# Query-major exponentials 384 wide with a quarter of the keys turned by DMA, the dP matmuls around the burst, and half of TensorE's turns by DMA

## The chip, the cores and the metric

The kernel runs on one core of one Trainium2 chip. The metric is the device time of one execution in microseconds. Three runs of the kernel before took 2671.75, 2677.37 and 2682.45 us.

## What is computed

The reference is a gated mix of a multi-head attention block and a state-space convolution, forward and backward: the output and the gradients of twelve inputs. The change touches the attention alone:

```python
B, S, D, H = 1, 2048, 576, 32          # Dh = 18
scores = jnp.einsum("bhqd,bhkd->bhqk", q, k) * (Dh ** -0.5)
p = _softmax(scores, axis=-1)
o = jnp.einsum("bhqk,bhkd->bhqd", p, v)
# backward (vjp): dv = p^T do;  dp = do v^T;  ds = p * (dp - delta);  dq = ds k;  dk = ds^T q
```

## The kernel before

The program has three stretches: projections, norms and gates (to about 123 us of the span); the attention loop, forward and backward (123 to 2087 us); and the convolution's gradients with the output matmuls (to the end). The engines' order is written by hand: the schedule is manual, each engine runs its instructions in the order in which the code issues them, and engines meet only at semaphores.

Attention works on 8 groups of 4 heads and 4 blocks of 512 queries: 32 units (g, b). The loop `for G in range(NTOT + OFF + 24)` takes 32 steps for a unit (NTOT = 1024 steps of forward work); the backward work of a unit follows its forward work by OFF = 39 steps, so that one step holds forward work of one unit and backward work of an earlier one. G2 = G - OFF counts the backward steps. A step does:

- P1: two matmuls on 32 rows of the array each (two heads), K against Q, give scores key-major, 128 keys x 512 queries a head. ACT takes the exponential of both at once (128x1024) into a tile PT. PT feeds the output matmuls accO (four heads, every other step) and, 39 steps later, ds.
- P3: the same scores for the backward unit once more, but query-major: 128 queries x 512 keys, two heads. ACT takes their exponential (128x1024) into eb. eb feeds dV.
- P2: two matmuls V against dO give dP, one head each into a PSUM tile of its own (two buffers, tag dP). DVE multiplies each by PT into ds (key-major, 128x512 a head, four heads to a tile).
- a burst: per eight steps (one key block of 512 keys, kq) a dV burst in two halves (steps slot 0 and 1; 16 matmuls from eb, first a filler matmul), a dQ burst in two halves (slots 2 and 3; from ds), a dK burst in two halves (slots 5 and 6; from dsT), and in slots 4 and 7 a turn on TensorE. All of them write one PSUM buffer (tag accB), which DVE empties after each second half or turn (`evs`).

dK needs ds with queries on the partitions, dsT. Heads 0 to 2 of each ds tile are turned by a DMA transpose that SP issues (line L1406); the fourth head is turned by TensorE against the identity (turn_p, L1097) and copied by DVE (L1102) for most tiles. `by_pe(p)` says how many of the two tiles of pair p (p = 0 to 7 in a unit) TensorE turns:

```python
return {NPF: 0, NPF + 1: 1}.get(p, 2)
```

With NPF = 5 that is 2, 2, 2, 2, 2, 0, 1, 2: 13 of a unit's 16 tiles.
Where TensorE turns the fourth head the DMA turn is 128x1536, else 128x2048. The two PSUM tiles of tag S (two buffers of two banks) alternate between P1 and P3, so P1 of a step waits for the exponential of P1 of the step before, and P3 likewise.

Beside this, SP's queue issues the loads of K, V, Q and their turned forms, and the turns gT of finished gradients (one of dQ a unit, eight of dV and dK in the last unit of a group). POOL runs the basis of the convolution throughout the loop (et, eG, eT, Eo and the store E_d; about the same amount a step, by a table of estimated costs), and, for the attention, dOa and prod once a unit and the packing of finished gradients (dtk, dqkv_d). DVE's reduce (L1057) waits once a unit for POOL's prod, and POOL's dOa for DVE's reciprocal rl.

Of the kernel before, what the change touches and what calls it, by code (L numbers as in the profile page):

```python
# [11 lines left out]
BF = mybir.dt.bfloat16  # L12
# [5 lines left out]
P = 128  # L18


def build(tc, aps, dbg_aps=None, stages=("s1", "attn", "post", "s4", "final")):
# [40 lines left out]
    with ExitStack() as gctx:  # L62
# [63 lines left out]
        woT = [eds.tile([P, 2, 512], BF, tag="eb", bufs=8, name="eb").rearrange("p a b -> p (a b)")[:, 0:D] for _ in range(DC)]  # L126
# [823 lines left out]
        if "attn" in stages:  # L950
            KB = 512
            NQ = S // KB
            TPQ = KB // P
            DA = HP
            NFILL = {"V": 1, "Q": 0, "K": 0}
            with ExitStack() as ctx:
                ctx.enter_context(tc.manual_schedule(engines={mybir.EngineType.PE, mybir.EngineType.Activation, mybir.EngineType.DVE, mybir.EngineType.Pool, mybir.EngineType.SP}))
# [177 lines left out]

                def dv_half(g, b, kq, h, acc):
                    U = UN[(g, b)]
                    for ii in (2 * h, 2 * h + 1):
                        for j in range(4):
                            mm(acc[HP * j:HP * (j + 1), :], lhsT=U["dOa"][:, ii, j, :], rhs=U["eb"].pop((kq, ii, j)),  # L1140
                               start=(ii == 0), stop=(ii == 3), tile_position=(0, HP * j))

                    def ev():
                        if b == 0:
                            DKV[("v", g, kq)] = work.tile([P, KB], F32, tag="dvacc", bufs=4, name="dvacc")
                            nc.vector.tensor_copy(DKV[("v", g, kq)], acc)
# [4 lines left out]
                        nc.vector.tensor_tensor(o_, a_, acc, op=A.add)  # L1151
                    return ev
# [136 lines left out]
                for G in range(NTOT + OFF + 24):  # L1289
# [18 lines left out]
                    if r1:  # L1308
                        g, b, i, j0 = r1
                        T = grp_t[g]  # L1310
                        ps = s_pair("P1")
                        for x in range(2):
                            row(ps[:, x, :], T["KaT", i // TPQ][:, (i % TPQ) * P:(i % TPQ + 1) * P], T["QaT", b], j0 + x)
                        rows.append(("P1", g, b, i, j0, ps))
                    evs = []
                    slot = (G2 + 1) % 8
                    m_ = (G2 - (7, 8, 8, 8, 8, 8, 8, 0)[slot]) // 8
                    if ("f1", G) in todo:
                        acc = accB("accF")
                        evs.append(todo.pop(("f1", G))[0](acc))  # L1320
                        e_done[0] += 1.4
                    elif G == NST + 5:
                        evs.append(turn(*do_tile(UN[units[0]])))
                    elif 0 <= m_ < NTOT // 8:
                        u_, kq = divmod(m_, NQ)
                        g, b = units[u_]
                        if slot in SLOTS:
                            nm, burst, h = SLOTS[slot]
                            if h == 0:
                                acc = accB("acc" + nm)  # L1330
                                fill(acc, NFILL[nm])
                                burst(g, b, kq, 0, acc)
                            else:
                                evs.append(burst(g, b, kq, 1, acc))
                                if nm == "Q" and kq == NQ - 1:
                                    at(("pre", G + 2), lambda g=g, b=b: store_grad(UN[(g, b)].pop("dqa"), g, 0, b * TPQ))
                                elif nm in "KV" and b == NQ - 1:
                                    at(("pre", G + 2), lambda g=g, kq=kq, nm=nm: store_grad(DKV.pop((nm.lower(), g, kq)), g, 1 + "KV".index(nm), kq * TPQ))
                        else:
# [5 lines left out]
                            evs.append(turn(t_, o_))  # L1345
                    if r2:
                        g, b, s2 = r2
                        T = grp_t[g]
# [8 lines left out]
                        i2 = s2 // 2  # L1357
                        for x in range(2):
                            j2 = 2 * (1 - par_) + x
                            ps = apsp.tile([P, KB], F32, tag="dP", bufs=2, name="ps_P2")  # L1360
                            row(ps, T["VaT", i2 // TPQ][:, (i2 % TPQ) * P:(i2 % TPQ + 1) * P], U["dOaT"].rearrange("p t q -> p (t q)"), j2)
                            rows.append(("P2", g, b, i2, j2, ps))
# [16 lines left out]
                    if 1 <= G <= 2 * NT:  # L1379
                        do_half(G - 1)  # L1380

                    for e_ in evs:
                        e_()
                    for (kind, g, b, i, j, ps) in rows:
                        U = UN[(g, b)]
                        if kind == "P1":
                            U["PT"][i, j // 2] = pt_tile()
                            nc.scalar.activation(U["PT"][i, j // 2], ps, ACT.Exp)  # L1388
                        elif kind == "P3":
                            e = eds.tile([P, 2, KB], BF, tag="eb", bufs=8, name="eb")  # L1390
                            for x in range(2):
                                U["eb"][(i[0], i[1], j + x)] = e[:, x, :]
                            nc.scalar.activation(e, ps, ACT.Exp)  # L1393
                        else:
                            if i not in U["ds"]:
                                U["ds"][i] = eds.tile([P, 4, KB], BF, tag="ds", bufs=5, name="ds")
                                U["dsn", i] = 0
                            nc.vector.tensor_tensor(U["ds"][i][:, j, :], ps, U["PT"][i, j // 2][:, j % 2, :], op=A.mult)  # L1398
                            U["dsn", i] += 1
                            nj = 3 if by_pe(i // 2) >= 2 - i % 2 else 4  # L1400
                            if U["dsn", i] == nj:
                                p = i // 2
# [472 lines left out]
```

## Time and profile before

| | |
|---|---|
| Median of three runs (range) | 2677.37 us (2671.75 to 2682.45) |
| Profiled execution, first to last instruction (span) | 2673.6 us; its own time outside the profiler is not listed apart |
| Mean granted TensorE clock | 0.968 |
| PE, DVE, ACT, POOL busy | 2405.5, 2294.7, 2352.0, 1830.1 us |
| eb and PT exponentials | 1024 each; 1070 and 1075 ns |
| ds multiplies (DVE) | 2048; 683 ns |
| DMA | 486.63 MB, 182 GB/s |

The span is what the sums are made against; it lies 3.8 us under the median. Times in the profile are microseconds, or ns for the mean of one instruction; "<-" stands between output and inputs; "idle before" is the engine's idle time ahead of such instructions, and what ended it. A recorded instruction overlaps its neighbour on the same engine somewhat, so that a mean duration is longer than the pace.

### The profile page before, as it was taken

How to read it: one execution, taken by the hardware profiler on the slowest of the kernel's cores; microseconds unless marked ns; L12 is line 12 of the kernel's file. 1: busy time of each engine (PE TensorE's matmuls, PEld its weight loads, DVE VectorE, ACT ScalarE, POOL GpSimd, SP SyncE). 2: the span in 40 equal slices, each digit the busy share in tenths (PEclk: the TensorE clock that was granted, in tenths of full speed). 3: DMA queues.
4: the chain of work that ended last, by engine and by line, in shares of the span. 5: the costliest groups of instructions: out<-in, count | busy, mean ns of one | idle time of the engine just before them, and what ended most of it. 6: DMA issues, size and time to landing. Idle time of an engine off the chain costs nothing.

```text
span 2673.6 us, 69952 instructions
## 1 busy us (share of the span) xinstructions
PE 2405.5 (90%) x27411; PEld 1134.6 (42%) x27411; DVE 2294.7 (86%) x4090; ACT 2352.0 (88%) x2744; POOL 1830.1 (68%) x2845
## 2 busy tenths in 40 slices
PE   8999999998889898889898999989988699999999
PEld 4433333333333333333333333333232489998756
DVE  5748999999889999889899999999897499999964
ACT  5589999999999999999999999999996489999321
POOL 0388878888888888888878888887931135555431
PEclk9989999999999999999999999999896699999999
DMA  7747889879979978997898899779668979998996
GB/s 232 202 114 152 150 171 177 162 156 181 169 151 172 185 157 163 173 167 152 165 179 157 157 172 169 154 164 181 134 136 174 224 229 262 260 263 250 269 255 136
DMA packets 1155478, 486.63 MB, mean 182 GB/s; under 512 B 1071062, under 2 KB 1108551, under 8 KB 1152843
## 3 DMA queue, kind: packets, MB, share of 16 engines
q1 hardware_dynamic: 1108346, 339.13, 64.3%
q0 software_dynamic: 44784, 137.52, 19.2%
q10 hardware_dynamic: 2016, 5.51, 0.7%
q8 instruction: 214, 3.51, 0.6%
q14 instruction: 118, 0.96, 0.1%
HBM read 146.27 MB, written 93.80 MB: 90 GB/s over the span
## 4 chain that ended last, share of the span: by engine, by line
ACT 39%; PE 28%; DVE 22%; issue 6%; DMA 3%; POOL 2%; SPq 1%; ACTq 0%; DVEq 0%; POOLq 0%
ACT eb L1393 23%; ACT PT L1388 14%; PE ps_P L30 8%; DVE ds L1398 7%; DVE tz L733 3%; DVE wab L753 3%; PE accV L30 2%; PE ps_dx L30 2%; PE turn_p L1097 2%; DVE tz L736 2%; PE accK L30 2%; DVE HG L738 2%; PE yp L30 2%; DVE Rw L758 1%; DVE dvacc L1151 1%
## 5 line engine op out<-in xcount | busy, mean ns | idle before, releaser
L1398 DVE TENSOR_TENSOR ds<-ps_P,PT 128x512 bf16<-128x512 f32 x2048 | 1312.5, 683 | 127.8 <-PE ps_P L30 87.3
L1393 ACT ACTIVATE eb<-ps_P 128x1024 bf16<-128x1024 f32 x1024 | 1095.7, 1070 | 44.3 <-PE ps_P L30 44.2
L1388 ACT ACTIVATE PT<-ps_P 128x1024 bf16<-128x1024 f32 x1024 | 1099.6, 1075 | 11.0 <-PE ps_P L30 9.5
L30 PE MATMUL ps_P<-dOaT,VaT_g 32*128 32x512 bf16 x2048 | 583.1, 390 | 30.8 <-DVE ds L1398 15.4
L506 POOL TENSOR_TENSOR et<-eG,eT 128x448 f32<-128x448 f32 x576 | 542.9, 963 | 10.7
L30 PE MATMUL ps_P<-QaT_g,KaT_g 32*128 32x512 bf16 x2048 | 404.7, 387 | 126.6 <-ACT PT L1388 122.2
L30 PE MATMUL ps_P<-KaT_g,QaT_g 32*128 32x512 bf16 x2048 | 408.9, 392 | 2.0 <-ACT eb L1393 1.4
L506 POOL TENSOR_TENSOR Eo<-et,et 128x448 bf16<-128x448 f32 x288 | 327.2, 1136 | 20.8
L30 PEld LDWEIGHTS <-KaT_g 32*128 32x128 bf16 x2048 | 147.4, 91 | 456.1 <-issue 438.2
L30 PEld LDWEIGHTS <-QaT_g 32*128 32x128 bf16 x2048 | 115.7, 91 | 288.6 <-issue 266.7
L30 PE MATMUL accV<-eb,dOa 128*32 128x512 bf16 x2048 | 185.6, 396 | 26.8 <-ACT eb L1393 26.5
L30 PE MATMUL accO<-PT,Vtok_g 128*32 128x512 bf16 x2048 | 207.9, 395 | 0.1
L30 PE MATMUL accK<-dsT,Qtok_g 128*32 128x256 bf16 x4096 | 165.3, 283 | 21.3 <-DMA dsT<-ds 19.9
L30 PE MATMUL accQ<-ds,Ktok_g 128*32 128x512 bf16 x2048 | 161.9, 394 | 2.2 <-DVE dvacc L1151 1.9
L30 PEld LDWEIGHTS <-Vtok_g 128*32 128x32 bf16 x2048 | 52.8, 93 | 222.6 <-issue 222.6
L1102 DVE COPY dsT<-turn_p 128x1024 bf16<-128x1024 bf16 (+1 forms) x216 | 139.2, 644 | 3.4 <-PE turn_p L1097 3.4
L1097 PE MATMUL turn_p<-ident_bf,ds 128*128 128x128 bf16 x1664 | 136.2, 225 | 1.4 <-DVE gb L1169 0.8
L672 ACT COPY E1e<-etp 128x1024 bf16<-128x1024 bf16 x132 | 125.4, 1063 | 2.7 <-PE etp L671 2.7
L30 PEld LDWEIGHTS <-Qtok_g 128*32 128x32 bf16 x4096 | 88.6, 97 | 87.8 <-issue 57.9
L506 POOL TENSOR_TENSOR et<-eT 128x32 f32<-128x32 f32 (+3 forms) x288 | 116.2, 424 | 11.4
L1097 PEld LDWEIGHTS <-ds 128*128 128x128 bf16 x1664 | 98.9, 100 | 50.2 <-issue 50.0
L1075 POOL COPY dtk<-gT 128x288 bf16<-128x288 bf16 x96 | 40.9, 426 | 107.6 <-DMA dqkv_d<-dtk 47.2
(295 smaller groups left out, 3731.0 us busy)
## 6 DMA issues: line engine op xcount, KB each, us to landing
E_d<-Eo POOLq DMA_DIRECT2D x144, 256.0 KB, 3.3
E1n<-E_d POOLq DMA_DIRECT2D x30, 1024.0 KB, 6.6
T0w<-Kp_d SPq DMA_DIRECT2D x18, 1024.0 KB
xs<-xb_d POOLq DMA_DIRECT2D x28, 512.0 KB, 9.9
dsT<-ds SPq DMA_TRANSPOSE x512
dqkv_d<-dtk POOLq DMA_DIRECT2D x96, 72.0 KB, 4.3
Md_d<-mst SPq DMA_DIRECT2D x18, 288.0 KB
skw<-Md_d SPq DMA_DIRECT2D x72, 64.0 KB
```

What stands on the lines that cost most here:

```text
L30: return nc.tensor.matmul(out, lhsT=lhsT, rhs=rhs, start=start, stop=stop, **kw)
L506: nc.gpsimd.tensor_tensor(out, a, b, op=op)
L672: copy(E_[:, 4 * q:4 * q + 4], pt_)
L733: nc.vector.tensor_tensor(tz[x], HG[:, :, k - 1].unsqueeze(1).to_broadcast([P, 2, 2, n, CB]), ZZ.unsqueeze(3).to_broadcast([P, 2, 2, n, CB ...
L736: nc.vector.tensor_tensor(tz[x][:, 0], tz[x][:, 0], UVk[:, :, :, k, :], op=A.add)
L738: nc.vector.tensor_tensor(HG[:, :, k], tz[x][:, 0], tz[x][:, 1, ::-1], op=A.add)
L753: nc.vector.tensor_tensor(wab, h_, w_, op=A.mult)
L1097: nc.tensor.transpose(pt_[:, x, qb, :], t_[:, qb * P:(qb + 1) * P], ident_bf)
L1102: (nc.scalar.copy if NTOT <= now[0] < NTOT + OFF else nc.vector.tensor_copy)(o_(), pt_[:, x:x + n])
L1388: nc.scalar.activation(U["PT"][i, j // 2], ps, ACT.Exp)
L1393: nc.scalar.activation(e, ps, ACT.Exp)
L1398: nc.vector.tensor_tensor(U["ds"][i][:, j, :], ps, U["PT"][i, j // 2][:, j % 2, :], op=A.mult)
```

## The change

It does four things. P3 and its exponential cover the first 384 of each 512 keys (KT); the last 128 keys of a block come from the forward's PT tile of those keys, which SP turns by DMA into PTt (two turns a key block, each 128x1024 for two heads; two buffers), issued at the start of steps G2 = 8 kq + 1 and + 2. The dV burst takes both: 384 columns from eb and 128 from PTt. The two dP matmuls of a step are split: the first goes ahead of the burst, right behind P1, the second stays after P3; on DVE the burst's eviction goes between the two multiplies. And `by_pe` lets TensorE turn only tiles of even pairs (7 of 16 a unit), the rest goes by DMA.

```diff
-        woT = [eds.tile([P, 2, 512], BF, tag="eb", ...)[:, 0:D] for _ in range(DC)]
-        dO_st = [eds.tile([P, 2, 512], BF, tag="eb", bufs=8, name="eb") for _ in range(3)]
+        woT = [eds.tile([P, 2, 384], BF, tag="eb", ...)[:, 0:D] for _ in range(DC)]
+        dO_st = [eds.tile([P, 2, 384], BF, tag="eb", bufs=8, name="eb") for _ in range(3)]
...
+            KT = KB - P
+            TURNED = (0, 1)
...
-                    return {NPF: 0, NPF + 1: 1}.get(p, 2)
+                    return {NPF + 1: 1}.get(p, 2) if p % 2 == 0 else 0
...
+                def turn_p(u, kq, pair):
+                    U = UN[u]
+                    t_ = U["PTt", kq, pair] = work.tile([P, 2 * TPQ, P], BF, tag="PTt", bufs=2, name="PTt")
+                    nc.sync.dma_start_transpose(out=t_, in_=U["PT"][kq * TPQ + 3, pair].rearrange("p x q -> p (x q)"))
...
                 def dv_half(g, b, kq, h, acc):
-                    for ii in (2 * h, 2 * h + 1):
+                    def stored(ii):
                         for j in range(4):
-                            mm(acc[HP * j:HP * (j + 1), :], lhsT=U["dOa"][:, ii, j, :], rhs=U["eb"].pop((kq, ii, j)),
+                            mm(acc[HP * j:HP * (j + 1), 0:KT], lhsT=U["dOa"][:, ii, j, :], rhs=U["eb"].pop((kq, ii, j)),
                                start=(ii == 0), stop=(ii == 3), tile_position=(0, HP * j))
+                    def turned(ii):
+                        for j in range(4):
+                            mm(acc[HP * j:HP * (j + 1), KT:KB], lhsT=U["dOa"][:, ii, j, :], rhs=U["PTt", kq, j // 2][:, j % 2 * TPQ + ii, :],
+                               start=False, stop=False, tile_position=(0, HP * j))
+                    stored(2 * h)
+                    turned(2 * h)
+                    turned(2 * h + 1)
+                    stored(2 * h + 1)
...
+                for u_ in range(NU):
+                    for kq_ in range(NQ):
+                        for x_, pair_ in enumerate(TURNED):
+                            at(("pre", u_ * NST + OFF + 8 * kq_ + 1 + x_), lambda u_=u_, kq_=kq_, pair_=pair_: turn_p(units[u_], kq_, pair_))
...
+                    if r2:
+                        p2(0)
                     evs = []
...
-                            row(ps[:, x, :], T["QaT", b][:, ii * P:(ii + 1) * P], T["KaT", kq], jo + x)
+                            row(ps[:, x, 0:KT], T["QaT", b][:, ii * P:(ii + 1) * P], T["KaT", kq][:, 0:KT], jo + x)
                         rows.append(("P3", g, b, (kq, ii), jo, ps))
...
+                        p2(1)
...
-                            e = eds.tile([P, 2, KB], BF, tag="eb", bufs=8, name="eb")
+                            e = eds.tile([P, 2, KT], BF, tag="eb", bufs=8, name="eb")
-                            nc.scalar.activation(e, ps, ACT.Exp)
+                            nc.scalar.activation(e, ps[:, :, 0:KT], ACT.Exp)
...
                             nc.vector.tensor_tensor(U["ds"][i][:, j, :], ps, U["PT"][i, j // 2][:, j % 2, :], op=A.mult)
+                            if j % 2 == 0:
+                                for e_ in evs:
+                                    e_()
```

How it moves instructions, at three places. On TensorE, in the first step with backward work (ps_P is a score or dP tile; "<-KaT_g,QaT_g" after QaT_g weights is P3, "<-dOaT,VaT_g" is P2):

```order
-L30 LDWEIGHTS QaT_g
-L30 MATMUL ps_P_1941<-KaT_g,QaT_g 128x512
-L30 LDWEIGHTS QaT_g
-L30 MATMUL ps_P_1941<-KaT_g,QaT_g 128x512
-L30 LDWEIGHTS VaT_g
-L30 MATMUL ps_P_1944<-dOaT,VaT_g 128x512
+L30 LDWEIGHTS VaT_g
+L30 MATMUL ps_P_1941<-dOaT,VaT_g 128x512
+L30 LDWEIGHTS QaT_g
+L30 MATMUL ps_P_1943<-KaT_g,QaT_g 128x384
+L30 LDWEIGHTS QaT_g
+L30 MATMUL ps_P_1943<-KaT_g,QaT_g 128x384
```

One dP matmul has moved ahead of the P3 pair (and, where there is a burst, ahead of it), and the pair is 384 wide.

On DVE, from the eviction of a dV burst to the turn four steps on, before:

```order
L1398 TENSOR_TENSOR ds<-ps_P_11227,PT 128x512
L1146 COPY dvacc<-accV 128x512
L1398 TENSOR_TENSOR ds<-ps_P_11250,PT 128x512
L1398 TENSOR_TENSOR ds<-ps_P_11252,PT 128x512
L1398 TENSOR_TENSOR ds<-ps_P_11285,PT 128x512
L1398 TENSOR_TENSOR ds<-ps_P_11287,PT 128x512
L1164 TENSOR_SCALAR dqa<-accQ 128x512
L1398 TENSOR_TENSOR ds<-ps_P_11319,PT 128x512
L1398 TENSOR_TENSOR ds<-ps_P_11321,PT 128x512
L1102 COPY dsT<-turn_p 128x2x512
```

And in the changed kernel:

```order
L1425 TENSOR_TENSOR ds<-ps_P_11651,PT 128x512
L1163 COPY dvacc<-accV 128x512
L1425 TENSOR_TENSOR ds<-ps_P_11672,PT 128x512
L1425 TENSOR_TENSOR ds<-ps_P_11695,PT 128x512
L1425 TENSOR_TENSOR ds<-ps_P_11709,PT 128x512
L1425 TENSOR_TENSOR ds<-ps_P_11732,PT 128x512
L1181 TENSOR_SCALAR dqa<-accQ 128x512
L1425 TENSOR_TENSOR ds<-ps_P_11745,PT 128x512
L1425 TENSOR_TENSOR ds<-ps_P_11765,PT 128x512
L1425 TENSOR_TENSOR ds<-ps_P_11770,PT 128x512
```

Each eviction now stands between the two multiplies of its step (11651 and 11672), and the copy of the turn in slot 4 is gone.

On SP, over some twelve steps of one unit, before (a ds tile of 12 blocks is three heads, of 16 four; x is the number in a row):

```order
L1071 DMA_TRANSPOSE gT<-gb 128x4x128
L1406 DMA_TRANSPOSE dsT<-ds 128x12x128 x3
L993 DMA KaT_g<-QKV_d 128x1x512
L1006 DMA QaT_g<-QKV_d 128x512
L1406 DMA_TRANSPOSE dsT<-ds 128x12x128 x4
L1010 DMA_TRANSPOSE Qtok_g<-QKV_d 128x4x128
```

And in the changed kernel:

```order
L1073 DMA_TRANSPOSE gT<-gb 128x4x128
L1436 DMA_TRANSPOSE dsT<-ds 128x16x128 x2
L1116 DMA_TRANSPOSE PTt<-PT 128x8x128
L1436 DMA_TRANSPOSE dsT<-ds 128x12x128
L1116 DMA_TRANSPOSE PTt<-PT 128x8x128
L995 DMA KaT_g<-QKV_d 128x1x512
L1008 DMA QaT_g<-QKV_d 128x512
L1436 DMA_TRANSPOSE dsT<-ds 128x12x128
L1436 DMA_TRANSPOSE dsT<-ds 128x16x128 x2
L1116 DMA_TRANSPOSE PTt<-PT 128x8x128
L1436 DMA_TRANSPOSE dsT<-ds 128x12x128
L1012 DMA_TRANSPOSE Qtok_g<-QKV_d 128x4x128
```

SP's queue has the PTt turns between the ds turns, and half of the ds turns are wider.

More of the change, by code (lines that the diff above doesn't have):

```diff
@@ L125, in build @@
         d_aT = [eds.tile([P, 4, 512], BF, tag="ds", bufs=5, name="ds") for _ in range(DC)]
-        woT = [eds.tile([P, 2, 512], BF, tag="eb", bufs=8, name="eb").rearrange("p a b -> p (a b)")[:, 0:D] for _ in range(DC)]
-        dO_st = [eds.tile([P, 2, 512], BF, tag="eb", bufs=8, name="eb") for _ in range(3)]
+        woT = [eds.tile([P, 2, 384], BF, tag="eb", bufs=8, name="eb").rearrange("p a b -> p (a b)")[:, 0:D] for _ in range(DC)]
+        dO_st = [eds.tile([P, 2, 384], BF, tag="eb", bufs=8, name="eb") for _ in range(3)]
         with ExitStack() as ctx:
@@ L1314, in build, with p2 @@
                         rows.append(("P1", g, b, i, j0, ps))
+                    def p2(x):
+                        g, b, s2 = r2
+                        i2, j2 = s2 // 2, 2 * (1 - (s2 + OFF) % 2) + x
+                        ps = apsp.tile([P, KB], F32, tag="dP", bufs=2, name="ps_P2")
+                        row(ps, grp_t[g]["VaT", i2 // TPQ][:, (i2 % TPQ) * P:(i2 % TPQ + 1) * P], UN[(g, b)]["dOaT"].rearrange("p t q -> p (t q)"), j2)
+                        rows.append(("P2", g, b, i2, j2, ps))
+                    if r2:
+                        p2(0)
                     evs = []
@@ L1344, in build @@
                                 t_, o_ = t2 + t_, o2 + o_
-                            evs.append(turn(t_, o_))
+                            if t_:
+                                evs.append(turn(t_, o_))
                     if r2:
@@ L1354, in build @@
                         for x in range(2):
-                            row(ps[:, x, :], T["QaT", b][:, ii * P:(ii + 1) * P], T["KaT", kq], jo + x)
+                            row(ps[:, x, 0:KT], T["QaT", b][:, ii * P:(ii + 1) * P], T["KaT", kq][:, 0:KT], jo + x)
                         rows.append(("P3", g, b, (kq, ii), jo, ps))
[L1357 to L1362, printed above, removed]
+                        p2(1)
                     tail = []
@@ L1380, in build @@
                         do_half(G - 1)
-                    for e_ in evs:
-                        e_()
+                    if not r2:
+                        for e_ in evs:
+                            e_()
                     for (kind, g, b, i, j, ps) in rows:
@@ L1399, in build @@
                             U["dsn", i] += 1
+                            if j % 2 == 0:
+                                for e_ in evs:
+                                    e_()
                             nj = 3 if by_pe(i // 2) >= 2 - i % 2 else 4
```

## The prediction

> **What bounds the kernel now.** I read the slices first, then the chain, then a long stretch of the attention loop engine by engine, then each engine's waits, and the transfers last. A step is one pass of the loop over G; a unit is 32 steps.
>
> ```profile
> span 2673.6 us, 69952 instructions
> ...
> PE   8999999998889898889898999989988699999999
> ...
> DVE  5748999999889999889899999999897499999964
> ACT  5589999999999999999999999999996489999321
> POOL 0388878888888888888878888887931135555431
> PEclk9989999999999999999999999999896699999999
> ...
> ACT 39%; PE 28%; DVE 22%; issue 6%; DMA 3%; POOL 2%; SPq 1%; ACTq 0%; DVEq 0%; POOLq 0%
> ACT eb L1393 23%; ACT PT L1388 14%; PE ps_P L30 8%; DVE ds L1398 7%; DVE tz L733 3%; DVE wab L753 3%; PE accV L30 2%; PE ps_dx L30 2%; PE turn_p L1097 2%; DVE tz L736 2%; PE accK L30 2%; DVE HG L738 2%; PE yp L30 2%; DVE Rw L758 1%; DVE dvacc L1151 1%
> ```
>
> From the third slice to about the twenty-eighth ACT is full, and the chain gives its two exponentials 37% of the span. The next rows, of 300 to 1700 us, price a step: by engine, then by group.
>
> ```profile
> 300.00:1700.00 1400.00, 1259.27 (x13647) 440.39 (x13646) 1263.40 (x2083) 1395.97 (x1516) 1187.59 (x1934) 1.00 0.88 166
> 2000.00:2030.00 30.00, 26.08 (x224) 8.24 (x226) 24.92 (x42) 19.57 (x21) 1.36 (x2) 0.64 0.58 121
> 2030.00:2087.00 57.00, 41.98 (x411) 14.05 (x404) 36.94 (x60) 30.95 (x33) 7.90 (x15) 0.68 1.10 219
> ```
> ```profile
> L1393 ACT ACTIVATE eb<-ps_P 128x1024 bf16<-128x1024 f32 x758 | 813.4, 1073 | 3.8 <-PE ps_P L30 3.7
> L1398 DVE TENSOR_TENSOR ds<-ps_P,PT 128x512 bf16<-128x512 f32 x1516 | 971.6, 683 | 80.2 <-PE ps_P L30 54.3 <-issue 15.8 <-ACT PT L1388 1.0
> L1102 DVE COPY dsT<-turn_p 128x1024 bf16<-128x1024 bf16 x144 | 98.1, 681 | 0.7 <-PE turn_p L1097 0.7
> L30 PE MATMUL ps_P<-dOaT,VaT_g 32*128 32x512 bf16 x1516 | 425.6, 381 | 22.5 <-DVE ds L1398 10.5
> L30 PE MATMUL ps_P<-QaT_g,KaT_g 32*128 32x512 bf16 x1516 | 296.1, 381 | 96.1 <-ACT PT L1388 94.1 <-DMA dsT<-ds 0.3
> L30 PE MATMUL accV<-eb,dOa 128*32 128x512 bf16 x1520 | 134.7, 387 | 19.0 <-ACT eb L1393 19.0
> ```
>
> In a row of a stretch the five busy times are PE, weight load, DVE, ACT, POOL, then the granted clock, the DMA share and GB/s. One eb exponential is a step, so 758 steps took 1400 us: 1.847 us a step, 59.1 a unit. ACT is busy 1396 of the 1400. Behind it stand DVE, 1263.4/758 = 1.667 us, and PE, which sat idle 22.5 + 96.1 + 19.0 = 137.6 us: (1400 - 137.6)/758 = 1.665. POOL looks free at 1187.6 us busy, but its waits say more:
>
> ```profile
> POOL dOa L1049 <- DVE rl L1044: 65.1, 19, 5.1
> POOL E_d L559 <- POOL Eo L506: 32.4, 109, 0.3
> POOL dtk L1075 <- DMA dqkv_d<-dtk: 27.5, 16, 5.2
> POOL dqkv_d L1076 <- POOL dtk L1075: 23.4, 72, 1.0
> POOL dtk L1075 <- DMA gT<-dvacc: 2.8, 2, 1.8
> ```
>
> Only 65.1 + 27.5 + 2.8 = 95.4 us of its idle time waits for another engine or a transfer; the rest is its own issue time and pauses between its instructions. POOL's own work is thus (1400 - 95.4)/758 = 1.721 us a step, the nearest floor under ACT.
>
> **The change, part by part.** *Exponentials 768 wide instead of 1024.* The one row of the same shape of work with another width:
>
> ```profile
> L708 ACT ACTIVATE UV<-uvp 128x512 bf16<-128x512 f32 x144 | 75.6, 619 | 8.8 <-PE uvp L30 8.6
> ```
>
> Between 619 ns for 512 and 1073 for 1024, 256 columns are 0.22 us. ACT falls from 1.842 (1396/758) to 1.62 us a step. If nothing else limited, that would be 0.22 x 985 steps with both exponentials = 217 us.
>
> *Score matmuls.* The query-major rows shrink from 512 to 384 columns, but each pair now runs beside one 512-wide dP matmul on other rows of the array, so PE gains nothing I can count; the first dP matmul of a step moves in front of the burst, beside the P1 pair. DVE can then multiply one half before it needs the burst. The eviction of the burst now stands in front of the second half: queued behind it are that multiply, the four-head turn of the tile on SP, and, on PE, the second dP matmul of the next step, which needs the same PSUM buffer.
>
> *The dV burst.* Per key block, 16 matmuls of 512 become 16 of 384 and 16 of 128. The columns are the same; 16 more instructions lie between nothing and the price of a small matmul:
>
> ```profile
> 1036.36 0.62 PE L30 MATMUL accQ<-ds,Ktok_g 128*32 128x512 bf16 x8
> ...
> 1039.82 0.62 PE L30 MATMUL accK<-dsT,Qtok_g 128*32 128x256 bf16 x16
> ```
>
> Sixteen narrow ones took what eight wide ones took, so up to 0.62/16 = 0.04 us each, at most 0.62 per eight steps, 0.08 us a step. I take the upper end: the record shows issue, not columns, as the limit there.
>
> *PE's turns.* 13 of a unit's 64 128x512 pieces of ds go through PE; now 7. That removes 24 matmuls a unit, and three wide copies on DVE: 3 x 0.681/32 = 0.064 us a step. DVE falls to 1.60.
>
> ```profile
> L1097 PE MATMUL turn_p<-ident_bf,ds 128*128 128x128 bf16 x1244 | 98.6, 221 | 0.0
> ```
>
> At 98.6/1244 = 0.079 us each PE saves 24 x 0.079/32 = 0.06 a step, about what the dV burst adds. PE stays near 1.67.
>
> *What SP and the DMA engines get.* Six such pieces a unit join the DMA turns (seven turns of 12 blocks and nine of 16, instead of thirteen and three), and eight turns PTt<-PT of 8 blocks come new. Each stands in SP's one queue; PT is some 33 steps old by then, and PTt is wanted five to six steps later, so its only wait is for the dV burst of the step before, which frees its two buffers.
>
> ```profile
> L1406 SPq DMA_TRANSPOSE dsT<-ds x379: 1274/1511/5387, 302.4 to 1699.7; - x190
> L1071 SPq DMA_TRANSPOSE gT<-dvacc x24: 1216/1234/4376, 373.8 to 1602.6; - x24
> L1010 SPq DMA_TRANSPOSE Vtok_g<-QKV_d x24: 1211/1276/2152, 307.7 to 1534.7; - x24
> ```
> ```profile
> 1056.58 0.58 SPq L1058 DMA_DIRECT2D O_d<-Ob  x1
> 1058.70 1.40 SPq L1406 DMA_TRANSPOSE dsT<-ds  x1
> ```
>
> The columns of the first fence are min/median/max in ns. A 12-block turn held SP 1.40 us; by size a 16-block one is at most 1.87; an 8-block one lies between 1.22 (4 blocks) and 1.51, say 1.40. A unit's other load is about three gT turns (1.24), three of tokens (1.28) and five plain loads (0.58): 10.5 us. Before: 13 x 1.40 + 3 x 1.87 + 10.5 = 34.3 of 59.1 us. After: 7 x 1.40 + 9 x 1.87 + 8 x 1.40 + 10.5 = 48.3, or 1.51 us a step. Below the floors, but close.
>
> This is where the Trainium skill speaks against the change. "Perfetto Trace Analysis", section "What DMA-bound means", counts a kernel as DMA-bound when the issuing engine's track is solid DMA slices; by that rule SP, at 48 of some 56 us, is nearly the bound, and the trace of before (34 of 59) cannot show that yet. "Advanced Engine Details and Errata", section "X-Bar Transpose (TRN2)", expects 350 to 400 GB/s of such turns; the row above, 128 x 1536 x 2 bytes in 1.40 us, is 281 GB/s for the issue, and by the page's figure the four-head turn would be an estimated 1.3 to 1.5 us, and SP some 36 us a unit. The measured row decides.
>
> ```profile
> q1 hardware_dynamic: 742192, 189.89, 75.1%
> q0 software_dynamic: 15455, 40.39, 12.4%
> ```
>
> The engines themselves: q1's packets are 256 bytes (189.89 MB/742192), so a 128x512 tile is 512 of them. A unit (1400/59.1 = 23.7 of them) had 31,300 and gains 6 x 512 + 8 x 1024 = 11,264, 36%. Lower bound, by the 1.40 us turn (1536 packets, 1097 per us): 42,600/1097 = 38.8 us, with q0's 12.4% of 59.1 (7.3 us) 46 us a unit, 1.44 a step. Upper bound: shares scale, 75.1 x 1.36 + 12.4 = 114.5% of 1.847 us; the fullest stretch above shows 1.10, so 1.92 us a step. I take the lower end, because the share of 1.10 says that packets' times overlap.
>
> *The sum.* ACT 1.62, DVE 1.60, PE 1.67, POOL 1.72, SP 1.51, DMA 1.44. POOL's work is not touched, so 1.72 is the floor; its lateness would show as DVE waiting for prod once a unit. To it I add the waits that ACT covers today and that come late next: PE for eb (19.0) and for DVE's buffers (22.5), 41.5/758 = 0.055. That gives 1.776, a gain of 0.071 x 985 = 70 us. The last 64 of these steps run partly at a granted clock under 1 and get half: minus 2. The 39 first and 39 last steps, without the pair, and everything before and after the loop get nothing; their cover does not change. 2673.6 - 68 = 2606; the median of the runs stands 3.8 us above this span, so 2610.
>
> **The rivals.** (B) The added waits stay hidden and only POOL's floor counts: 1.721, 0.126 x 985 = 124 us, 2553. For it: PE and DVE have slack against 1.72. Against: four engines stand within 8% of each other, each running its instructions in order.
>
> (C) SP's queue takes ACT's place. It decides when the 24 turns average (59.1 - 10.5)/24 = 2.02 us; at 2.00 a step is 1.83, a gain of 17 us, 2660. For it: the longest dsT issue was 5.4 us, and each group's last unit has six more gT than the average: 48.3 + 6 x 1.24 = 55.7 us. Against: the medians.
>
> (D) The other side: the DMA engines are the bound at 1.92 us a step, 0.073 x 985 = 72 us slower, 2749. It decides as soon as the attainable share is under 114.5% of today's time. For it: the share is 0.88 already; against: the 1.40 us turn. PE would wait on dsT and PTt.
>
> The Trainium skill's sequencer rule above is rival C, as far as its mechanism goes.
>
> **How the numbers follow.** My forecast 0.52, B 0.15, C 0.17 (2650 to 2690), D 0.13, and 0.03 for a lower granted clock in the denser loop. The range 2548 to 2690 takes in B and C with the forecast; D and the tails are left out. A measurement of this kernel tells about 0.5% (13 us) from no change. Faster: 0.52 + 0.15 + 0.06 of C = 0.73; same: 0.08 of C + 0.02; slower: D, 0.03 of C, 0.01: 0.17. With the forecast alone: 2580 to 2635.
>
> **What would show it.** Right: eb rows near 845 ns; ACT no longer full between 300 and 1700 us; POOL's wait for rl gone and a new wait of DVE's reduce for prod; PTt turns of 1.3 to 1.5 us; POOL's busy share near 0.95. Wrong: ACT still full (then a step is 1.62 and POOL's floor was misread); PE waiting for dsT or PTt by tens of us (C or D), in D with dsT issues far above 1.5 us at the median; the granted clock under 1 in the loop.

## The result, and the profile after

The changed kernel took 2823.84 us (median of four runs, 2811.52 to 2855.92) against 2676.62 us for the kernel before on the same chip: a ratio of 1.053, 95% interval 1.0488 to 1.0573. It is 147 us slower; 67 us faster was forecast. The ratio goes by the three faster of the four executions; the profiled one is the slowest, 2855.92 us at a granted clock of 0.82 against 0.838 to 0.856, so its sums are some 1% above the median.

The page of the kernel after, its slices, one queue and its chain:

```profile
span 2854.2 us, 72923 instructions
...
PE   8999988887888789888888898988899489999999
...
ACT  5589878897898688889878887888796289999421
POOL 0388877886787767778867877787670125555421
PEclk9888868787787687768777877887786589999999
...
PE 49%; ACT 17%; DVE 16%; DMA 12%; issue 4%; SPq 2%; ACTq 0%; POOL 0%; DVEq 0%; POOLq 0%
```

ACT is no longer full in the loop, as forecast. But the chain has passed from ACT (39% before) to PE (49%) and to transfers (12%, before 3%), and the row of the granted clock, nearly all nines in the loop before, reads mostly 6 to 8. The stretch of 300 to 1700 us, and in it the groups of ACT and of the first dP matmuls:

```profile
300.00:1700.00 1400.00, 1220.35 (x13239) 413.51 (x13238) 1123.15 (x1825) 1168.01 (x1376) 1080.15 (x1765) 0.77 1.10 195
```
```profile
L1415 ACT ACTIVATE PT<-ps_P 128x1024 bf16<-128x1024 f32 x688 | 718.1, 1044 | 47.1 <-PE ps_P L30 46.6
L1420 ACT ACTIVATE eb<-ps_P 128x768 bf16<-128x768 f32 x688 | 573.2, 833 | 184.8 <-PE ps_P L30 181.6
L30 PE MATMUL ps_P<-dOaT,VaT_g 32*128 32x512 bf16 x1375 | 596.1, 459 | 0.2 <-DVE ds L1425 0.2
```

688 steps in 1400 us are 2.035 us a step, against 1.847. The difference times 985 steps is 185 us; the two spans differ by 2854.2 - 2673.6 = 180.6, so the loop holds the whole loss. ACT now waits 46.6 + 181.6 = 228 us for PE. PE has two complaints. One is the clock: 0.77, and since the clock record knows only 1.0 and 0.5 here, 2 x (1 - 0.77) = 46% of the time ran at half speed. The other is transfers, in the list of waits:

```profile
ACT eb L1420 <- PE ps_P L30: 181.6, 277, 7.5
POOL dOa L1051 <- DVE rl L1046: 132.6, 21, 16.2
PE accV L30 <- DMA PTt<-PT: 37.2, 17, 6.5
PE accK L30 <- DMA dsT<-ds: 29.1, 15, 3.6
```

The columns are us in total, times, and the longest. PE lost 66.3 us to late PTt and dsT. Before it was 2.4 us, almost all in this row:

```profile
PE accK L30 <- DMA dsT<-ds: 2.1, 2, 1.9
```

SP's turns and the DMA queue of the kernel after, in the same stretch:

```profile
L1436 SPq DMA_TRANSPOSE dsT<-ds x344: 1293/2026/6836, 298.9 to 1697.2; - x172
L1116 SPq DMA_TRANSPOSE PTt<-PT x171: 1231/1296/5031, 301.9 to 1686.8; - x171
```
```profile
q1 hardware_dynamic: 918464, 233.52, 98.1%
q0 software_dynamic: 14032, 36.77, 11.2%
```

The dsT turn's median rose from 1511 to 2026 ns. Part of that is the mix, since nine of sixteen are now 16 blocks wide instead of three; by size, over 300 to 1900 us, the medians went from 1.42 to 1.64 us (12 blocks) and from 1.68 to 2.38 (16 blocks). q1 rose from 75.1% to 98.1%: the hardware queue is full. Its packets a step are 918464/688 = 1335, before 742192/758 = 979: 36% more, as counted. But it moved only 918464/1400 = 656 packets a us.

What the clock does, in PE's timeline of the kernel after (start, duration, matmuls, and in brackets the idle time ahead with what ended it):

```profile
329.45 0.61 PE L30 MATMUL accQ<-ds,Ktok_g 128*32 128x512 bf16 x8
330.00 0.34 PE L30 MATMUL ps_P<-KaT_g,QaT_g 32*128 32x384 bf16 x2
330.00 0.39 PE L30 MATMUL ps_P<-dOaT,VaT_g 32*128 32x512 bf16 x1
330.75 0.39 PE L30 MATMUL ps_P<-QaT_g,KaT_g 32*128 32x512 bf16 x2 [0.36 <-ACT PT L1415]
330.76 0.39 PE L30 MATMUL ps_P<-dOaT,VaT_g 32*128 32x512 bf16 x1
331.45 0.34 PE L30 MATMUL ps_P<-KaT_g,QaT_g 32*128 32x384 bf16 x2 [0.31 <-ACT eb L1420]
331.58 0.37 PE L30 MATMUL ps_P<-dOaT,VaT_g 32*128 32x512 bf16 x1
332.37 0.61 PE L30 MATMUL ps_P<-QaT_g,KaT_g 32*128 32x512 bf16 x2 [0.41 <-ACT PT L1415]
332.38 0.60 PE L30 MATMUL ps_P<-dOaT,VaT_g 32*128 32x512 bf16 x1
332.91 1.05 PE L30 MATMUL accK<-dsT,Qtok_g 128*32 128x256 bf16 x16
333.88 0.50 PE L30 MATMUL ps_P<-KaT_g,QaT_g 32*128 32x384 bf16 x2
...
338.95 0.34 PE L30 MATMUL ps_P<-KaT_g,QaT_g 32*128 32x384 bf16 x2
```

After the second dQ half (329.45) comes slot 4, where TensorE now has no turn. PE has only the score matmuls there and waits for ACT three times, 0.36, 0.31 and 0.41 us. Then the same matmuls take 0.61 us instead of 0.39, and the dK half 1.05 instead of 0.62, until 338.95. No transfer was late here. The clock record puts this drop at 331.9 us, just before the third wait, 6.8 us long; its neighbours begin at 301.2, 318.3, 349.0 and 366.0. There are 66 drops between 300 and 1900 us (before: 2).

The second kind of drop stands in the trace of before, once, at a late dsT (PE's timeline, around slots 5 and 6):

```profile
1128.19 0.62 PE L30 MATMUL accK<-dsT,Qtok_g 128*32 128x256 bf16 x16
...
1132.01 1.05 PE L30 MATMUL accK<-dsT,Qtok_g 128*32 128x256 bf16 x16 [1.85 <-DMA dsT<-ds]
...
1137.93 0.39 PE L30 MATMUL ps_P<-KaT_g,QaT_g 32*128 32x512 bf16 x2
```

One wait of 1.85 us, and half speed until about 1137.9. The record puts the drop at 1130.9, 0.73 us into the wait.

So there were two suspects. **G**, the gap: with TensorE's turn gone from slot 4, PE's short waits lie close together and the clock falls by itself. **D**, the DMA turns: with PTt added, SP's queue and the DMA engines are full, PE waits for PTt and dsT, and the clock falls at each long wait. In the counts below, a drop is put down to a long wait if a gap of PE of over 0.9 us reaches into the 9 us ahead of it; these counts are over 300 to 1900 us, from the trace's records of instructions and clock.

### The profile page after: what moved, and what is told of

The parts are those of the page before. It is cut to its first block, busy times and chain, and to the rows that moved or that the text cites. A ratio compares the mean times of both kernels' runs of the same rounds, so it can differ in the third digit from the quotient of the medians.

```text
span 2854.2 us, 72923 instructions
## 1 busy us (share of the span) xinstructions
PE 2507.2 (88%) x28691; PEld 1159.1 (41%) x28691; DVE 2260.5 (79%) x3997; ACT 2195.2 (77%) x2741; POOL 1830.1 (64%) x2845
## 4 chain that ended last, share of the span: by engine, by line
PE 49%; ACT 17%; DVE 16%; DMA 12%; issue 4%; SPq 2%; ACTq 0%; POOL 0%; DVEq 0%; POOLq 0%
PE ps_P L30 16%; ACT eb L1420 8%; ACT PT L1415 7%; PE accV L30 6%; PE accK L30 6%; DVE ds L1425 5%; DMA PTt<-PT 5%; DMA dsT<-ds 5%; PE accO L30 5%; PE turn_p L1099 2%; DVE tz L733 2%; DVE wab L753 2%; PE ps_dx L30 2%; PE accQ L30 2%; PE yp L30 2%
## 5 line engine op out<-in xcount | busy, mean ns | idle before, releaser
L1420 ACT ACTIVATE eb<-ps_P 128x768 bf16<-128x768 f32 x1024 | 852.2, 833 | 304.6 <-PE ps_P L30 300.3
L30 PE MATMUL ps_P<-dOaT,VaT_g 32*128 32x512 bf16 x2048 | 884.2, 459 | 5.4 <-DVE ds L1425 5.2
L30 PE MATMUL ps_P<-QaT_g,KaT_g 32*128 32x512 bf16 x2048 | 516.4, 457 | 89.6 <-ACT PT L1415 82.4
L506 POOL TENSOR_TENSOR et<-eG,eT 128x448 f32<-128x448 f32 x576 | 542.8, 963 | 10.7
L30 PE MATMUL ps_P<-KaT_g,QaT_g 32*128 32x384 bf16 x2048 | 397.7, 384 | 31.7 <-ACT eb L1420 30.9
L30 PE MATMUL accK<-dsT,Qtok_g 128*32 128x256 bf16 x4096 | 215.9, 348 | 69.5 <-DMA dsT<-ds 61.5
L30 PE MATMUL accO<-PT,Vtok_g 128*32 128x512 bf16 x2048 | 247.3, 471 | 1.9 <-DMA Vtok_g<-QKV_d 1.7
L30 PE MATMUL accV<-eb,dOa 128*32 128x384 bf16 x2048 | 207.2, 397 | 16.1 <-ACT eb L1420 14.5
L30 PEld LDWEIGHTS <-dOa 128*32 128x32 bf16 x4096 | 92.8, 105 | 228.3 <-issue 217.9
L30 PEld LDWEIGHTS <-VaT_g 32*128 32x128 bf16 x2048 | 182.5, 94 | 5.9 <-issue 5.9
L30 PE MATMUL accV<-PTt,dOa 128*32 128x128 bf16 x2048 | 93.8, 252 | 55.7 <-DMA PTt<-PT 55.3
```

Of the source, the lines that this page charges most:

```text
L30: return nc.tensor.matmul(out, lhsT=lhsT, rhs=rhs, start=start, stop=stop, **kw)
L506: nc.gpsimd.tensor_tensor(out, a, b, op=op)
L1420: nc.scalar.activation(e, ps[:, :, 0:KT], ACT.Exp)
```

## The experiments

### Filler matmuls in the empty slot

The changed kernel, with two filler matmuls into a scratch tile where slot 4 (or 7) has no turn:

```diff
                             if t_:
                                 evs.append(turn(t_, o_))
+                            else:
+                                fill(accB("accX"), 2)
```

> The changed kernel with two filler matmuls (512 wide, 0.6 us together) in slot 4 of every eight steps, where TensorE no longer has a turn. Theory G (the granted clock falls because slot 4 leaves TensorE too little to do; half speed for about 7 us in every 14): mean clock of the span 0.93 or more, 2600 to 2720 us. Theory D (SP's queue and the DMA engines are late, TensorE waits for PTt and dsT, and the clock falls behind those waits): the waits for PTt and dsT stay near 100 us or grow, clock under 0.88, 2780 us or more.

Measured: 2806.15 us, ratio to before 1.0479 (1.0424 to 1.0533). Its stretch of 300 to 1700 us (703 steps, 1.991 us each), and PE's waits there:

```profile
300.00:1700.00 1400.00, 1185.43 (x13647) 405.67 (x13643) 1138.93 (x1866) 1174.16 (x1406) 1095.65 (x1787) 0.86 1.11 199
```
```profile
PE accV L30 <- DMA PTt<-PT: 63.2, 41, 3.8
PE accK L30 <- DMA dsT<-ds: 55.3, 23, 5.7
```

This is the outcome expected for D. The clock rose from 0.77 to 0.86, yet the step became only 0.044 us shorter, while PE's waits for transfers grew from 66.3 to 118.5 us. All 40 drops that are left have a long wait just ahead; in the changed kernel it was 18 of 66. The filler took away one kind of drop and left the other, and most of what it gave back went into the transfers. The 18 us between the two medians are not clear of the noise: the intervals of the two ratios overlap.

### Thirteen turns on TensorE again

The changed kernel with `by_pe` of before; the PTt turns stay.

```diff
-                    return {NPF + 1: 1}.get(p, 2) if p % 2 == 0 else 0
+                    return {NPF: 0, NPF + 1: 1}.get(p, 2)
```

> The changed kernel with TensorE's turns of before (13 of 16 tiles), the 384-wide exponentials, the PTt turns and the split dP matmuls kept. Theory G: slot 4 is full again, clock 0.93 or more, 2600 to 2690 us. Theory D: 6 x 512 of the 11264 added packets a unit go away, about a quarter, so TensorE's waits for transfers and the time lost fall by a quarter to a half: 2720 to 2790 us.

Measured: 2707.13 us, 1.0116 (1.008 to 1.0152). The stretch and the queue:

```profile
300.00:1700.00 1400.00, 1215.27 (x14806) 452.94 (x14802) 1226.80 (x2037) 1232.71 (x1482) 1155.50 (x1888) 0.89 1.12 197
```
```profile
q1 hardware_dynamic: 921135, 234.02, 99.2%
```

The time lies between the two ranges expected. On top of the rest of the change the fewer turns cost 2823.84 - 2707.13 = 117 us, of which the filler gave back 18: a turn on TensorE fills the slot and also keeps packets out of the queue. A step (741 of them, 1.889 us) has 1243 packets instead of 1335, at the same full queue and nearly the same rate, 658 a us.

### Only the fewer turns

The kernel before, with `by_pe` of the changed kernel and nothing else.

```diff
-                    return {NPF: 0, NPF + 1: 1}.get(p, 2)
+                    return {NPF + 1: 1}.get(p, 2) if p % 2 == 0 else 0
...
-                            evs.append(turn(t_, o_))
+                            if t_:
+                                evs.append(turn(t_, o_))
```

> The kernel before with half of TensorE's turns by DMA and nothing else changed. Theory G: slot 4 is empty while a step still takes ACT 1.84 us, so TensorE idles more than in the changed kernel and the clock falls: 0.80 to 0.93, 2690 to 2800 us. Theory D: q1 carries 10% more packets, SP has room, so the clock stays at 0.96 and the time at 2670 to 2690 us.

Measured: 2796.06 us, 1.0413 (1.0342 to 1.0484): some 120 us slower with the exponentials 512 wide and no PTt. The stretch (714 steps, 1.961 us) and the list of PE's waits in it, from the top:

```profile
300.00:1700.00 1400.00, 1251.81 (x12314) 399.67 (x12313) 1161.51 (x1896) 1335.80 (x1428) 1117.57 (x1813) 0.88 0.88 169
```
```profile
PE ps_P L30 <- ACT PT L1389: 59.6, 228, 0.5
PE ps_P L30 <- ACT eb L1394: 35.5, 67, 0.7
PE accV L30 <- ACT eb L1394: 23.0, 85, 0.6
PE ps_P L30 <- DVE ds L1399: 10.0, 47, 0.2
PE accK L30 <- DMA dsT<-ds: 3.1, 3, 1.9
```

The DMA share is 0.88 as before, and transfers cost PE 3.1 us, but the clock is 0.88. None of the 58 drops has a long wait ahead. This is G alone, as expected for it.

### The fewer turns, with filler

The same, with the filler of the first experiment in the `else` branch.

> The kernel before with half of TensorE's turns by DMA and two filler matmuls in the empty slot 4. Theory G: the 118 us that the half turns cost by themselves are the empty slot, so the clock is back at 0.95 or more and the time at 2670 to 2700 us. Rival (the wider DMA turns themselves cost it): 2760 us or more.

Measured: 2684.25 us, 1.004 (1.0021 to 1.0058), with the clock at 0.99 and five drops:

```profile
300.00:1700.00 1400.00, 1241.97 (x13134) 424.96 (x13131) 1222.06 (x2000) 1388.64 (x1507) 1179.86 (x1925) 0.99 0.96 178
```

Filler matmuls whose result is never used give back 112 us. What the turn did for the time was to keep PE at work.

### No PTt turns

The changed kernel without the PTt turns and without the matmuls that read PTt; everything else, the narrow exponential too, is there.

```diff
                     stored(2 * h)
-                    turned(2 * h)
-                    turned(2 * h + 1)
                     stored(2 * h + 1)
...
-                            at(("pre", u_ * NST + OFF + 8 * kq_ + 1 + x_), ... turn_p(units[u_], kq_, pair_))
+                            pass
```

> The changed kernel without the PTt turns and without the 128-wide matmuls that read them; this leaves out a quarter of dV's sum. Theory G: slot 4 stays empty, the dV burst is shorter still, so the clock stays under 0.88 and the time at 2740 us or more. Theory D: 8 x 1024 of the 11264 added packets a unit are gone, no wait for PTt is left, and the time falls to the sum of the prediction or below, 2560 to 2640 us.

Measured: 2708.15 us, 1.0117 (1.0079 to 1.0155). The stretch (739 steps, 1.894 us):

```profile
300.00:1700.00 1400.00, 1249.34 (x12747) 416.35 (x12743) 1204.36 (x1963) 1248.33 (x1479) 1154.81 (x1892) 0.81 0.94 175
```

The time lies in neither of the ranges expected. Transfers now cost PE 10.7 us, but the clock stays at 0.81: 76 drops, two with a long wait ahead. Leaving PTt out also leaves out the 16 narrow matmuls a key block that read it (93.8 us of PE in the page of the changed kernel), so this run prices the turns and those matmuls together.

### No PTt turns, and filler

Both together.

> The changed kernel without the PTt turns and their matmuls (a quarter of dV's sum left out), and with two filler matmuls in the empty slot 4: neither suspected cause is left. If both causes together are the whole loss (theory G + D), the clock is 0.95 or more and the loop runs at the floors of the prediction, 1.70 to 1.78 us a step, 2550 to 2620 us. Rival R (the narrower exponentials cannot be used at all, because TensorE, DVE and ACT are coupled step by step): 2650 us or more with few waits for transfers.

Measured: 2615.69 us, 0.9798 (0.9767 to 0.9828). The stretch (791 steps, 1.770 us), and waits of PE and DVE:

```profile
300.00:1700.00 1400.00, 1224.99 (x13794) 419.01 (x13793) 1271.16 (x2098) 1305.40 (x1582) 1231.57 (x2005) 0.94 1.00 186
```
```profile
PE accK L30 <- DMA dsT<-ds: 32.9, 15, 6.6
DVE ds L1425 <- PE ps_P L30: 47.4, 180, 0.9
DVE dOa L1059 <- POOL prod L1053: 22.7, 13, 2.9
```

With the empty slot and the PTt turns both out, the step is 1.770 us against the 1.776 of the forecast, and DVE's wait for POOL's prod is there that the forecast named. The time and the step lie in the ranges expected; the clock, 0.94, misses 0.95. Late transfers are not all gone: the wider dsT turns are still there, PE waits 32.9 us for them, and 15 of the 19 drops have a long wait ahead. The four kernels in a square, median us:

| | slot 4 empty | slot 4 filled |
|---|---|---|
| with PTt turns | 2823.84 | 2806.15 |
| without | 2708.15 | 2615.69 |

The filler is worth 18 us with the PTt turns and 92 without; the PTt turns and their matmuls cost 116 with the slot empty and 190 with it filled. The effects do not add, since each alone holds the step near 1.9 to 2.0 us; both have to go.

### Thirteen turns and no PTt

Both removed without any filler: `by_pe` of before, and no PTt.

> The changed kernel without the PTt turns and their matmuls (a quarter of dV's sum is left out) and with the 13 turns a unit on TensorE of before: neither of the two suspected causes is left. If they are the whole of the loss, the narrow exponential is seen alone: the clock near 1.0, dsT waits of PE near those of before (a few us), and 2553 (POOL's floor) to 2610 us. If narrowing the exponential by itself makes PE's idle gaps drop the clock, the clock stays under 0.95 and the time above 2640 us.

Measured: 2588.52 us, 0.9672 (0.9629 to 0.9714). The stretch (791 steps, in an execution of 2606.49 us) and DVE's waits:

```profile
300.00:1700.00 1400.00, 1252.85 (x14253) 445.82 (x14252) 1304.80 (x2176) 1310.36 (x1582) 1239.15 (x2013) 0.93 0.94 173
```
```profile
DVE ds L1423 <- PE ps_P L30: 40.3, 71, 0.9
DVE dOa L1059 <- POOL prod L1053: 34.5, 16, 4.5
```

The narrow exponential by itself, with its turned columns for nothing, is worth 90 us (2678.75 for before in this batch). PE's waits for dsT are 1.0 us here, yet the clock was 0.93, not near 1.0: the expectation holds on the time and misses on the clock. Of 23 drops eleven have a long wait ahead; PE's list over 300 to 1900 us shows 15 waits for DVE's ds, up to 5.0 us, where DVE itself stood waiting for prod. For the other drops no cause was isolated.

### Only the split dP matmuls

The kernel before with the split of P2 and the eviction between the two multiplies, at full width (`KT = KB`, `TURNED = ()`).

```diff
+            KT = KB
+            TURNED = ()
...
+                    if r2:
+                        p2(0)
...
+                            if j % 2 == 0:
+                                for e_ in evs:
+                                    e_()
```

> The kernel before with the dP matmuls split around the burst and the eviction between the two multiplies, nothing else. Theory G + D: no part in the loss; ACT stays the bound at 1.84 us a step, 2665 to 2690 us. Rival (the split itself spreads TensorE's work so that the clock falls): clock under 0.94, 2700 us or more.

Measured: 2675.33 us, 1.0008 (0.999 to 1.0027): nothing. Its stretch has the same 758 steps as before:

```profile
300.00:1700.00 1400.00, 1157.87 (x13614) 443.90 (x13614) 1281.03 (x2080) 1395.63 (x1515) 1185.70 (x1932) 0.99 0.88 166
```

PE is busy 101 us less than before at the same pace and the clock holds. Its idle time is this row of PE's waits:

```profile
PE ps_P L30 <- ACT PT L1413: 221.5, 641, 0.5
```

That is a third of a us each, spread at nearly one a step. So the sum of PE's idle time over the stretch does not drop the clock; what matters is how it falls (the last section).

### One pair of heads only

Thirteen turns, the split, and 384 columns with PTt for heads 0 and 1; heads 2 and 3 keep 512. That is four PTt turns a unit, with one PTt buffer instead of two and four eb buffers of each width instead of eight.

```diff
-            TURNED = (0, 1)
+            TURNED = (0,)
...
-                    return {NPF + 1: 1}.get(p, 2) if p % 2 == 0 else 0
+                    return {NPF: 0, NPF + 1: 1}.get(p, 2)
...
-                            e = eds.tile([P, 2, KT], BF, tag="eb", bufs=8, name="eb")
+                            w_ = KT if j // 2 in TURNED else KB
+                            e = eds.tile([P, 2, w_], BF, tag="eb" if w_ == KT else "ebw", bufs=4, name="eb")
```

> TensorE's turns of before, the dP matmuls split, and only the first pair of heads with 384-wide exponentials and PTt turns (4 a unit instead of 8); the second pair stays 512 wide. ACT's floor is 1.73 us a step. Theory D (the turns' lateness grows steeply near SP's limit): waits of TensorE for PTt and dsT under 30 us between 300 and 1900 us, clock 0.93 or more, 2600 to 2660 us. Rival (each PTt turn costs alike, half of what the eight cost): 2670 to 2700 us.

Measured: 2627.81 us, 0.9836 (0.9814 to 0.9857): 46 us faster than before. The stretch (775 steps, 1.806 us) and the queue:

```profile
300.00:1700.00 1400.00, 1186.61 (x14719) 474.58 (x14721) 1295.14 (x2129) 1352.84 (x1550) 1210.82 (x1980) 0.98 1.04 188
```
```profile
q1 hardware_dynamic: 859574, 218.97, 91.4%
```

1109 packets a step, and a queue with room left. Time and clock lie where they were expected for D, but PE still waits 37.0 us for dsT over 300 to 1900 us, where under 30 was expected. This is the version that beats both kernels.

### PTt turned two steps later

The filled kernel, and the one-pair kernel, each with the PTt turns at steps 8 kq + 3 and + 4 (one pair: + 3).

```diff
-at(("pre", u_ * NST + OFF + 8 * kq_ + 1 + x_), ...
+at(("pre", u_ * NST + OFF + 8 * kq_ + 3 + x_), ...
```

> The changed kernel with the filler in slot 4, and the PTt turns issued two steps later (steps 8 kq + 3 and + 4 instead of + 1 and + 2), which leaves them four steps ahead of the dV burst that needs them. If SP's late transfers come from SP standing idle in front of each PTt turn until its buffer is free (in the filled kernel about 190 us of such waits over 1600 us of span, with the dsT turns queued behind), most of that wait goes, the half-clock stretches behind waits for dsT and PTt become fewer, and the time falls from 2806 us to some 2700 or less. If the load itself (SP's issue time and the DMA engines' 1.11 share) is the limit, the place in the queue does not matter: 2780 to 2830 us, with the same share of waits for PTt and dsT.

> The version with one pair of heads at 384 columns (one PTt turn a key block) and 13 turns on TensorE, with the PTt turn issued two steps later. If the wait in front of the PTt turn is what delays dsT there, PE's 37 us of waiting for dsT shrinks and the time falls from 2628 us to about 2600. If the load is the limit: 2620 to 2635 us.

Measured: 2891.33 us for the filled kernel, 1.0798 (1.0769 to 1.0827), and 2653.3 us for the one-pair kernel, 0.9902 (0.9874 to 0.993). Both are slower than with the earlier place, by 0.032 and 0.007 in the ratio; both of the ways expected for each were wrong. PE's waits in the filled kernel, over 300 to 1900 us:

```profile
PE accV L30 <- DMA PTt<-PT: 150.1, 74, 6.2
...
PE accK L30 <- DMA dsT<-ds: 4.2, 3, 2.3
```

dsT is on time now and PTt pays. SP stood in front of the PTt turns as long as with the earlier place (196 us, before 194), so the edit moved that wait and did not shorten it; whether it is what makes dsT late was not settled. q1 had room here (93.8%), so a step of 2.065 us comes from lateness and not from the number of packets alone. Of the two places tried the earlier one is the better.

> The same as the one-pair version with the later PTt turn, plus two filler matmuls in the one slot a unit in which TensorE has no turn. If empty slots drop the granted clock one by one, the clock rises from 0.96 and the time falls by 5 to 15 us against the kernel without the filler; if a single empty slot in 32 steps is harmless (before has one too, at a clock of 1.0), within 5 us of it.

Measured: 2647.52 us, 0.9891 (0.9867 to 0.9916), the clock 0.97 with the filler as without. The intervals of the two overlap: no cost of a single empty slot in a unit is seen.

## Why the prediction was wrong, step by step

**The exponentials: right.** The eb rows came out at 833 ns for a forecast of 845, and ACT is no longer full. ACT's busy time is 1305.4/791 = 1.65 us a step without the PTt turns, against 1.62.

**"PE stays near 1.67": failed, through the clock.** The step counted a turn as 24 matmuls a unit saved and took the granted clock as unchanged. A turn was also what filled slot 4. With slot 4 empty and nothing else changed, the clock went to 0.88 and the kernel lost some 120 us; filler matmuls returned 112. A clock under 1 had 0.03 of the chances, with no time worked out. That PE at half speed paces the step is seen in the groups of after: both exponentials wait for it.

The Trainium skill, "TensorE: Matmul & The Clock Gate", section "HAM oscillation — how this bites in real kernels", gives as the rule that TensorE must have no idle gap above about 3.4 us. This case disagrees: with only the fewer turns, all 58 drops came with no gap above 0.9 us ahead. The Trainium skill, on the same page, section "A second HAM failure mode: psum-queue depth-cycling", says that frequent micro-idles can make the clock oscillate. The trace agrees: ahead of the drop at 331.9 us stand gaps of 0.36 and 0.31 us.

**SP's 48.3 us a unit: too low.** It was made of single or median issue times, from a queue with room; the means in the trace of before, over 300 to 1900 us, were already 1.64 us for a 12-block turn and 2.13 for 16 blocks, where 1.40 and 1.87 were taken. Means over 300 to 1900 us in the trace of after are 1.96 us for a 12-block turn, 2.46 for 16 blocks and 1.46 for PTt: 7 x 1.96 + 9 x 2.46 + 8 x 1.46 + 10.5 = 58 us, in a unit of 32 x 2.035 = 65. The 8-block price itself (1.40 taken, median 1.296, mean 1.46) was right.

**The DMA engines, "I take the lower end": failed.** The packets were right (36% more), the pace was not. The 1097 a us was one turn's packets over its issue time; with the queue full, three kernels ran at 656, 671 (939469/1400, the filled one) and 658. The trace of before had the number: 979 packets in 1.847 us are 530 a us at a share of 0.88, which scaled to the largest share that the forecast had seen, 1.10, gives 663. At 663 the changed kernel's 1335 packets are 2.01 us a step, and it took 2.035; the 1243 packets with thirteen turns are 1.87, and took 1.889. The upper bound, 1.92, was the better number, and rival D (0.13) names this mechanism; its 2749 us was 75 us too low, as even the upper bound was, and D did not have the clock.

**How the two combine.** Going from the changed kernel to the one with filler and no PTt, the step falls by 2.035 - 1.770 = 0.265 us. PE's waits for transfers are 66.3/688 - 32.9/791 = 0.055 of it. The other 0.21 comes with the time at half speed, 0.94 us a step (46% of 2.035) against 0.21 (12% of 1.770): 0.29 us lost for each us at half speed. From the kernel with fewer turns to the same with filler it is (1.961 - 1.859)/(0.24 x 1.961 - 0.02 x 1.859) = 0.24.

**POOL's floor and the added waits: right in size, partly by luck.** The step without both causes was 1.770 for 1.776, and DVE waits for prod. But POOL's share is 0.88 (1231.57/1400), not 0.95, and this kernel and the one with thirteen turns and no PTt still spent 12 and 14% of the time at half speed, a cost that the forecast did not have; by 0.24 to 0.29 it is some 0.05 to 0.07 us a step, about what was added for waits. In the changed kernel POOL's wait for rl did not go: it is 132.6 us, because the bound lay elsewhere.

**Split and eviction: right.** Costed at nothing, measured at nothing.

Of the signs that were listed as "wrong", ACT did not stay full; the other three appeared: waits for PTt and dsT of tens of us, dsT issues well above 1.5 us at the median, and a clock under 1 in the loop.

What stays open: whether SP's issues are longer because the DMA engines are full or would be late anyway (the two were not separated), and what beside PE's busy share in a window decides a drop (below).

## What to carry to other kernels

Before taking matmuls away from a TensorE that waits for another engine, look at the slot they leave: if the waits around it come close together, the clock can fall to half. Filler in that slot tells whether it did, provided that nothing else holds the step: with only the fewer turns it gave back 112 us, with the PTt turns on top 18. Price added transfers by packets a step over the rate that the engines reach in their fullest stretch, not by the rate of one transfer running alone. When two causes each hold the step at nearly the same length, removing one shows little; try them in a square of four kernels before judging either.

## What the runs showed of the hardware

- The clock changed only on a fixed grid: in each trace all its records begin at one phase of 3.413 us, to within 5 ns. What goes with a drop is how busy PE was in the grid window that ends there. In the changed kernel, over 300 to 1900 us and in windows at full clock, a busy share of 0.74 or less stood ahead of 54 of 65 drops and in only 2 of the 197 other windows. Over the fourteen traces it stood ahead of 364 of 411 drops, and in 120 of 5022 other windows.
- Short gaps are enough, if they fall into one window: ahead of the drop at 331.9 us the gaps are 0.19, 0.36 and 0.31 us, a share of 0.75. The 1.85 us wait in the trace of before counted with the 0.73 us that lay ahead of the grid point, a share of 0.74.
- The share is not the whole rule: with only the split, nine windows at 0.69 ended in a drop, and 32 of the 449 others stood at 0.70 or less without one.
- A stretch at half speed lasted a whole number of 3.41 us: of the 66 in the changed kernel three took 3.41 us, 38 took 6.83, eight 10.24, and the longest 51.2.
- Over 300 to 1700 us no kernel passed a DMA share of 1.12; the three with the queue at 98 to 99% stood at 1.10 to 1.12, at 656 to 671 packets of some 256 bytes a us.
- A DMA turn of 8 blocks never held SP for less than 1.23 us, about as long as the shortest of 4 blocks (1.19), and one of 12 or 16 never for less than 1.27.
